# Another order of all steps in a fused linear-attention and gated-MLP kernel, with additions and products exchanged between VectorE and GpSimd

## The chip, the cores and the metric

The kernel runs on one core of a Trainium2 chip. A core has five engines with queues of their own: TensorE (PE in the profile, its weight loads PEld), VectorE (DVE), ScalarE (ACT), GpSimd (POOL) and SyncE (SP), which here issues all DMAs. Each engine works through its own instructions in the order in which they were written, and waits on semaphores for the others. The metric is the time of one launch on the device in microseconds; what is compared is the median of several runs.

## The reference

Eight batches, eight heads, a sequence of 576, heads of 64, a model width of 512 and an MLP of 1024 hidden columns. First a linear attention, with a softmax of q along a head's channels and one of k along the sequence:

```python
q_s = np.exp(q - np.max(q, axis=-1, keepdims=True))
q_s = q_s / (np.sum(q_s, axis=-1, keepdims=True) + 1e-09)
k_s = np.exp(k - np.max(k, axis=2, keepdims=True))
k_s = k_s / (np.sum(k_s, axis=2, keepdims=True) + 1e-09)
kv = np.einsum('bhsd,bhse->bhde', k_s, v)
x = np.einsum('bhsd,bhde->bhse', q_s, kv)      # then heads side by side: 576 x 512
```

Then an MLP with a spatial gate, in float32:

```python
h = x @ w_in
h = 0.5 * h * (1.0 + np.tanh(c * (h + 0.044715 * h ** 3)))
u, v = h[..., :512], h[..., 512:]
v_n = (v - mu) / np.sqrt(var + 1e-06) * g_ln    # mu, var: mean and variance of v's row
v_s = np.einsum('ts,bsd->btd', w_sg, v_n) + b_sg[None, :, None]
out = x + (u * v_s) @ w_out
```

## The kernel before, in words

**Steps and plan.** The kernel is a set of small functions, called steps, and one long text, PLAN, which names all 1254 calls of them in the order in which they are issued. A step's numbers say which piece it works on, most often the batch and then a half, a column block or a row block. A letter at the end chooses the engine where there is a choice: V for VectorE, A for ScalarE, G for GpSimd; without a letter the step's default holds. `InOrder` (line 139) wraps SyncE, VectorE, ScalarE and GpSimd so that each keeps the order of the plan, and `mm` (line 234) does the same for TensorE. So the plan sets the order on every engine, and there is no other scheduler. All instructions of the four wrapped engines carry line 149 in the profile, and all matmuls line 235: groups are told apart by the names of their tiles.

**Precision.** A product in full precision is made of three in a faster format: every operand is split into a high part (suffix _h or _high) and the rest (_l or _low), and high x high, high x low and low x high are summed in PSUM. So each intermediate has a step for its high part (a copy on ScalarE) and one for its low part (a subtraction).

**The stages.** For a batch b:
- k: `load_k`, the maximum over the sequence (`k_ma`, `k_mb`, `k_mc`, then a transpose on TensorE `kt_mm`, `k_top`, and a transpose back `kb_mm`), `k_sub`, `k_exp`; then `kv_mm` with v, `kv_inv` and `kv_scale`. Halves of four heads each.
- q: `load_q`, `q_max`, `q_swapm`, `q_top`, `q_sub`, `q_exp`, `q_sum`, `q_swapd`, `q_inv`, `q_mul`, `q_turn`. A head's 64 channels lie on two groups of 32 partitions; the swaps are four small copies that exchange the maxima (`q_swapm`) or the sums (`q_swapd`) between neighbouring groups. `q_sub` subtracts the maximum, `q_mul` multiplies by the inverse sum, `q_turn` transposes blocks on VectorE.
- x: `x_mm` from kv and q, `x_high` (ScalarE), `x_low` (VectorE).
- The MLP: `hv_mm` (5 row blocks; the tails of two batches share one) with `hv_gelu`, `hv_stat`, `hv_pow`, `hv_norm`, `hv_high`, `hv_low`; `hu_mm` with `hu_gelu`; `sg_mm` over the sequence, `gate`, `gate_high`, `gate_low`; `out_mm`, `out_add`, `out_rest`, `out_store`.

Batch 0 has steps of its own (`k0_...`, `q0_...`, `x0_...`, `hu0_mm`), which work on smaller pieces so as to begin early. Before its MLP the weights must be converted from 64-bit words to the two parts: `wi_a` (ScalarE), `wi_b`, `wi_c`, `wi_d` (VectorE), `wi_h` (ScalarE) and `wi_l`, for eight column blocks of w_in; the same with `wo_` for four blocks of w_out; `ws_h` and `ws_l` for five blocks of w_sg. `wi_x` and `ws_x` let TensorE make the low part where ScalarE then copies it out. The last column block of batch 7 is done in two halves by `last_mm`, `last_add`, `last_rest`, `last_store`.

**Buffers.** PSUM holds three double banks, used in turn (`bank`, line 222) by the x, hu, sg and out products, and two single ones for hv, kv, kt and kb. A step that writes a bank waits until the one three (or two) before it has been read out. q, k and v have two buffers each (one for each half of the heads), so a load waits for the batch before: `load_k` and `load_v` for its `kv_mm`, `load_q` for its `q_turn`. SyncE issues all loads and stores in one queue, and those behind a waiting one wait too.

**Activation tables.** ScalarE's exp steps and gelu steps need different tables; where one kind follows the other in ScalarE's order, a table load stands between them (ACT_TABLE_LOAD in the profile).

## Time and profile before

| | before |
|---|---|
| median of 3 runs | 523.53 us (522.45 to 524.46) |
| the profiled execution | 523.98 us, span of its instructions 522.2 us |
| TensorE busy | 491.4 us (94%), 3862 matmuls |
| VectorE busy | 355.9 us (68%) |
| ScalarE busy | 245.0 us (47%) |
| GpSimd busy | 166.7 us (32%) |
| DMA | 48.74 MB, mean 93 GB/s |

The profile is one execution, with every instruction's start, duration, and, where an engine sat idle before it, what ended the wait. A row of a timeline reads: start, duration, engine, line, operation, tile written <- tiles read, shapes, count, and in brackets the idle time before it with its releaser. A row of a group reads: line, engine, operation, tiles, shapes, count | busy us, mean ns of one | idle time before, and who ended most of it.

### The profile page before, as it was taken

Reading aid. Unit: us, or ns where it says so; the run is one execution under the profiler, and the core shown is the slowest. Engines: PE = TensorE matmul, PEld = TensorE weight load, DVE = VectorE, ACT = ScalarE, POOL = GpSimd, SP = SyncE. Lnnn points to the kernel's source line nnn. Section 1 sums busy time; section 2 is a strip of 40 time slices with the busy share of each in tenths; the row PEclk is TensorE's granted clock in tenths of the full one; section 3 lists DMA queues with packets and bytes.
Section 4 is the critical chain, followed back from the end, with each engine's and each line's share of the span. In section 5 each row is a group of like instructions: output and inputs, shape, how many; then the busy total and the mean of one; then the engine's idle time right before and its main releaser. Section 6 shows DMA issues by size and latency. Waiting matters only on the chain.

```text
span 522.2 us, 9404 instructions
## 1 busy us (share of the span) xinstructions
PE 491.4 (94%) x3862; PEld 447.4 (86%) x3862; DVE 355.9 (68%) x596; ACT 245.0 (47%) x445; POOL 166.7 (32%) x199
## 2 busy tenths in 40 slices
...
GB/s 284 379 279 268 146 150 1 2 187 87 68 130 121 46 137 0 2 102 120 143 1 109 226 75 0 1 1 112 178 97 23 3 68 1 1 0 46 1 17 119
DMA packets 19630, 48.74 MB, mean 93 GB/s; under 512 B 1666, under 2 KB 8196, under 8 KB 19588
## 3 DMA queue, kind: packets, MB, share of 16 engines
...
## 4 chain that ended last, share of the span: by engine, by line
PE 71%; DVE 16%; ACT 5%; DMA 4%; issue 1%; POOL 1%; SPq 1%; ACTq 0%; DVEq 0%; POOLq 0%
PE ps L235 71%; DVE qd L149 3%; DVE ot_i L149 2%; DMA raw_x_l<-w_out 2%; DVE km L149 1%; DVE v L149 1%; DVE qt L149 1%; DMA kk<-k 1%; DVE o L149 1%; DVE ot_o L149 1%; DVE vnl L149 1%; DMA ukt<-k 1%; DVE kk L149 1%; DVE qm L149 1%; ACT v L149 1%
## 5 line engine op out<-in xcount | busy, mean ns | idle before, releaser
L149 POOL TENSOR_TENSOR rs<-ve,half 128x1 f32<-128x1 f32 x36 | 28.9, 810 | 97.0 <-DVE ve L149 94.9
L235 PE MATMUL ps<-ulow,wo_h 128*128 128x288 f32 x256 | 55.7, 296 | 1.1 <-DVE ulow L149 1.1
L235 PE MATMUL ps<-ws_h,vnh 128*128 128x288 f32 x256 | 56.0, 300 | 0.0
L235 PE MATMUL ps<-gh,wo_h 128*128 128x288 f32 x256 | 56.0, 298 | 0.0
L235 PE MATMUL ps<-ws_h,vnl 128*128 128x288 f32 x256 | 55.0, 296 | 0.7 <-DVE vnl L149 0.7
L235 PE MATMUL ps<-gh,wo_l 128*128 128x288 f32 x256 | 55.4, 295 | 0.0
L235 PE MATMUL ps<-ws_l,vnh 128*128 128x288 f32 x256 | 54.8, 295 | 0.0
L149 DVE TENSOR_TENSOR u<-ps,u 128x576 f32<-128x576 f32 x32 | 24.1, 754 | 42.5 <-PE ps L235 34.0
L149 ACT ACT_TABLE_LOAD x28 | 35.9, 1283 | 32.2 <-PE ps L235 21.1
L149 POOL TENSOR_TENSOR ulow<-u,gh 128x576 fp32r<-128x576 f32 x15 | 21.9, 1459 | 91.2 <-DVE ulow L149 46.1
L149 ACT ACTIVATE u<-ps 128x576 f32<-128x576 f32 (+1 forms) x36 | 21.2, 599 | 62.3 <-PE ps L235 62.0
L235 PEld LDWEIGHTS ps<-ws_h,vnh 128*128 128x128 f32 x256 | 41.2, 188 | 2.2 <-DVE u L149 1.8
L235 PEld LDWEIGHTS ps<-ulow,wo_h 128*128 128x128 f32 x256 | 41.2, 188 | 1.6 <-DVE ulow L149 1.3
L235 PE MATMUL ps<-x_h,wi_h 128*128 128x288 f32 x256 | 41.8, 303 | 0.8 <-DVE x_l L149 0.8
L235 PEld LDWEIGHTS ps<-ws_h,vnl 128*128 128x128 f32 x256 | 41.2, 188 | 1.1 <-DVE vnl L149 1.1
L235 PE MATMUL ps<-wi_h,x_h 128*128 128x512 f32 x144 | 40.2, 400 | 1.9 <-DVE kk L149 1.5
L235 PEld LDWEIGHTS ps<-gh,wo_h 128*128 128x128 f32 x256 | 41.3, 188 | 0.6
L235 PEld LDWEIGHTS ps<-ws_l,vnh 128*128 128x128 f32 x256 | 41.3, 188 | 0.0
L235 PEld LDWEIGHTS ps<-gh,wo_l 128*128 128x128 f32 x256 | 41.3, 188 | 0.0
L149 DVE TENSOR_TENSOR o<-ps,x_h 128x576 f32<-128x576 f32 (+1 forms) x33 | 23.7, 730 | 25.4 <-PE ps L235 21.7
L149 ACT ACTIVATE v<-ps 128x512 f32<-128x512 f32 x36 | 21.5, 597 | 40.3 <-PE ps L235 36.8
L235 PEld LDWEIGHTS ps<-x_h,wi_h 128*128 128x128 f32 x256 | 36.0, 190 | 5.0 <-DVE x_l L149 1.7
...
## 6 DMA issues: line engine op xcount, KB each, us to landing
...
```

Of the source, the lines that this page charges most:

```text
L149: ins = op(*args, **kw)
L235: tc.keep_in_program_order(nc.tensor.matmul(*args, **kw))
```

## The change

The plan is replaced by another order of the same 1254 steps; no step is added or left out, and no function changes. 65 of the steps also change their engine:

| steps | from | to | count |
|---|---|---|---|
| `wi_l` 3, 4, 6; `wo_l` 2; `ws_l` 1, 2, 4 | GpSimd | VectorE | 7 |
| `out_rest` | GpSimd | VectorE | 7 |
| `out_rest` | VectorE | GpSimd | 5 |
| `gate_low` | GpSimd | VectorE | 5 |
| `gate_low` | VectorE | GpSimd | 10 |
| `q_mul`, `q0_mul` | GpSimd | VectorE | 6 |
| `q_mul` | VectorE | GpSimd | 5 |
| `q_sub`, `q0_sub` | GpSimd | VectorE | 3 |
| `q_sub` | VectorE | GpSimd | 2 |
| `q_swapm`, `q_swapd`, and q0's (six of these in batch 0) | GpSimd | ScalarE | 12 |
| `q_swapm` 2 0 and 3 1, `q_swapd` 3 1 | ScalarE | GpSimd | 3 |

The diff, cut to the head (up to the first `hu_mm`), one stretch of the middle and the tail:

```diff
...
-load_q0 1 0, q0_max 1 0, load_q0 0 0, q0_max 0 0, load_k0 3, q0_swapm 1 0 G, q0_top 1 0, q0_sub 1 0, load_k0 0, k0_max 3, k0_exp 3, q0_exp 1 0
-k0_max 0, load_q0 1 1, q0_max 1 1, q0_swapm 0 0 G, q0_top 0 0, q0_sub 0 0, q0_sum 1 0, load_q0 0 1, q0_max 0 1, load_k0 2, k0_max 2, load_b, b_h
-q0_swapd 1 0 G, q0_inv 1 0, q0_exp 0 0, q0_sum 0 0, load_eye, q0_swapm 0 1 G, q0_top 0 1, load_w_in 3, wi_a 3, wi_b 3, k0_exp 2, q0_mul 1 0, load_k0 1
-k0_exp 0, k0_max 1, k0_mm 0, q0_swapm 1 1 G, q0_turn 2 0, wi_c 3, k0_exp 1, q0_top 1 1, q0_turn 3 0, load_w_in 1, wi_a 1, wi_b 1, load_w_in 0
-k0_copy 0, wi_a 0, q0_swapd 0 0 G, q0_inv 0 0, k0_mm 1, q0_sub 1 1, wi_d 3, k0_mm 2, load_v 0 1, wi_b 0, k0_copy 2, load_v 0 0, wi_c 1, wi_c 0
-q0_sub 0 1, k0_mm 3, k0_copy 3, q0_exp 0 1, load_w_in 2, q0_sum 0 1, k0_copy 1, load_w_in 5, wi_d 1, load_w_in 7, q0_exp 1 1, kv_mm 0 1, kv_mm 0 0
-kv_inv 0 1, q0_mul 0 0, wi_h 1, wi_d 0, kv_scale 0 1, load_w_in 4, x0_mm 1 0, neg, kv_inv 0 0, wi_a 2, q0_sum 1 1, q0_swapd 0 1 G, wi_b 2, wi_h 0
-wi_x 0, wi_h 3, q0_inv 0 1, x0_high 1 0, x0_neg 1 0, wi_l 1, load_w_sg 3, load_k 1 0, wi_c 2, wi_l 3, wi_a 7, wi_a 5, kv_scale 0 0, q0_mul 0 1
-q0_turn 0 0, q0_turn 1 0, wi_d 2, x0_mm 0 0, wi_h 2, q0_turn 1 1, wi_x 2, x0_high 0 0, x0_neg 0 0, wi_b 5, q0_swapd 1 1 G, x0_low 1 0 A, load_k 1 1
-q0_inv 1 1, q0_mul 1 1, wi_b 7, load_w_in 6, x0_low 0 0 A, q0_turn 0 1, wi_l 0 A, load_w_sg 0, hu0_mm 1 0, load_q 1 0, hu0_gelu 1 0, hu0_mm 3 0
-wi_c 5, wi_a 6, q0_turn 3 1, q0_turn 2 1, load_q 1 1, k_ma 1 0, load_w_out 1, load_v 1 0, hu0_gelu 3 0, x0_mm 1 1, wi_c 7, load_g, wi_a 4
-load_w_out 0, wi_d 5, x0_mm 0 1, x0_high 0 1, hu0_mm 0 0, x0_high 1 1, x0_neg 1 1, load_w_out 2, x0_neg 0 1, wi_h 5, load_w_out 3, wi_x 5
-x0_low 1 1 A, wi_l 2 A, ws_h 0, load_w_sg 1, wi_l 5 A, b_l, k_mb 1 0, x0_low 0 1 A, k_mc 1 0, kt_mm 1 0, hu0_mm 2 0, q_max 1 0, wi_d 7, wi_h 7, wi_x 7
-k_ma 1 1, wo_a 1, k_top 1 0, kb_mm 1 0, hu0_gelu 0 0, k_mb 1 1, wi_b 4, k_mc 1 1, wi_c 4, hu0_gelu 2 0, q_max 1 1, ws_x 0, load_w_sg 4, q_swapm 1 0 G
-load_w_sg 2, wi_l 7 A, q_top 1 0, wi_b 6, k_sub 1 0, kt_mm 1 1, k_top 1 1, wi_d 4, q_swapm 1 1 G, wo_b 1, q_top 1 1, k_exp 1 0, wi_c 6, wi_d 6
-q_sub 1 0, q_exp 1 0, ws_l 0 A, hu0_mm 2 1, wi_h 6, kb_mm 1 1, k_sub 1 1, wi_h 4, q_sub 1 1, hu0_mm 0 1, q_exp 1 1, q_sum 1 0, q_swapd 1 0, q_sum 1 1
-kv_mm 1 0, wi_l 6, wi_l 4, wo_a 3, kv_inv 1 0, wo_a 0, hu0_mm 1 1, hv_mm 0 1, q_inv 1 0, kv_scale 1 0, wo_b 3, wo_c 3, q_swapd 1 1 G, q_inv 1 1
-wo_b 0, k_exp 1 1, hv_gelu 0 1, wo_c 1, hv_mm 0 3, hv_gelu 0 3, wo_a 2, load_v 2 0, load_v 1 1, kv_mm 1 1, load_k 2 1, q_mul 1 0 1, q_turn 1 1, wo_d 1
-q_mul 1 0 0, wo_c 0, ws_h 3, wo_d 0, hu0_gelu 2 1, kv_inv 1 1, hu0_gelu 0 1, load_k 2 0, q_mul 1 1 0, hv_mm 0 0, hv_gelu 0 0 A, q_turn 1 0, x_mm 1 0
-x_high 1 0, q_mul 1 1 1, x_high 1 1, kv_scale 1 1, wo_b 2, ws_h 2, hu0_gelu 1 1, load_q 2 0, q_turn 1 2, q_turn 1 3, wo_d 3, load_q 2 1, hv_mm 0 2
-wo_c 2, wo_d 2, x_low 1 0, hv_gelu 0 2 A, x_mm 1 1, x_high 1 3, x_high 1 2, x_low 1 1, hv_stat 0 1, hv_norm 0 1, x_low 1 3, wo_h 0, hu0_mm 3 1
-x_low 1 2, hv_pow 0 1, ws_h 4, hv_stat 0 3, hv_mm 0 4, hv_high 0 1, hv_low 0 1, hv_pow 0 3, hv_sq 0 0, hv_mm 1 1, hv_gelu 0 4 A, hv_norm 0 0
-hv_sq 0 2, ws_h 1, hv_stat 0 0 A, hv_mm 1 3, hv_norm 0 3, hv_high 0 3, hv_pow 0 0, ws_l 3 V, hv_low 0 3, hv_sq 0 4, hv_norm 0 4, hv_stat 0 2 A
-hv_gelu 1 1 A, hv_stat 0 4 A, hv_high 0 0, hv_sq 1 1, hv_low 0 0, ws_l 4, hv_pow 0 2, hv_pow 0 4, hv_gelu 1 3, q_max 2 1, k_ma 2 1, hv_norm 0 2
-ws_l 2, hv_mm 1 2, q_max 2 0, ws_l 1, wo_h 1, hv_high 0 2, tail_high 1, hv_low 0 2, tail_high 0, tail_again 0, hu0_gelu 3 1, k_ma 2 0, k_mb 2 0
-hv_gelu 1 2 A, k_mb 2 1, k_mc 2 1, tail_low 0, q_swapm 2 1, hv_stat 1 1 A, wo_h 3, hv_stat 1 3, q_swapm 2 0, q_top 2 0, q_sub 2 0 V, hv_mm 1 0
-tail_low 1, q_top 2 1, hv_gelu 1 0 A, load_v 2 1, k_mc 2 0, q_sub 2 1, q_exp 2 1, sg_mm 0 0, gate 0 0, hv_sq 1 2, kt_mm 2 1, sg_mm 0 2, kt_mm 2 0
-k_top 2 1, kb_mm 2 1, k_top 2 0, wo_l 1, gate 0 2, sg_mm 0 3, hv_norm 1 1, kb_mm 2 0, gate_high 0 0, k_sub 2 1, k_exp 2 1, k_sub 2 0, sg_mm 0 1
-gate 0 1, hu_mm 1 0, hv_norm 1 3, hv_sq 1 0, gate_high 0 2, gate 0 3, gate_high 0 1, wo_h 2, wo_l 0 V, hv_stat 1 0 A, kv_mm 2 1, load_k 3 1, k_exp 2 0
...
-gate 7 0, hu_gelu 7 3, sg_mm 7 1, gate_high 7 0, gate_low 7 0 G, hu_mm 7 1, hu_gelu 7 1, gate 7 1, gate_high 7 1, gate_low 7 1, sg_mm 7 2, sg_mm 7 3
-gate 7 2, gate 7 3, gate_high 7 2, out_store 6 0, gate_high 7 3, gate_low 7 2, gate_low 7 3, out_rest 6 2 V, out_store 6 2, out_mm 7 2, out_add 7 2
-last_mm 7 0, out_mm 7 1, out_rest 6 1, out_store 6 1, last_add 7 0, last_rest 7 0, last_store 7 0, out_add 7 1, out_rest 7 2 V, last_mm 7 1
-last_add 7 1, last_rest 7 1, out_mm 7 0, out_rest 7 1 V, out_store 7 1, last_store 7 1, out_add 7 0, out_store 7 2, out_rest 7 0 V, out_store 7 0
+load_k0 0, k0_max 0, load_q0 0 1, q0_max 0 1, k0_exp 0, q0_swapm 0 1, q0_top 0 1, q0_sub 0 1, load_eye, q0_exp 0 1, load_q0 1 1, load_q0 0 0
+q0_max 1 1, q0_max 0 0, load_w_in 3, q0_swapm 1 1 G, q0_top 1 1, q0_sum 0 1, q0_sub 1 1, q0_swapm 0 0, load_q0 1 0, k0_mm 0, q0_max 1 0, q0_top 0 0
+q0_sub 0 0 V, q0_swapd 0 1, wi_a 3, wi_b 3, load_k0 1, q0_inv 0 1, q0_mul 0 1, q0_exp 0 0, neg, q0_exp 1 1, q0_sum 0 0, q0_swapd 0 0 G, load_w_in 2
+wi_a 2, load_k0 3, k0_max 1, k0_exp 1, q0_sum 1 1, k0_copy 0, q0_inv 0 0, load_v 0 0, wi_c 3, q0_swapm 1 0, k0_mm 1, load_k0 2, load_w_in 1, k0_max 3
+k0_copy 1, k0_exp 3, q0_turn 1 1, wi_b 2, q0_top 1 0, kv_mm 0 0, k0_mm 3, k0_max 2, q0_turn 0 1, kv_inv 0 0, wi_a 1, load_w_sg 0, q0_swapd 1 1
+k0_exp 2, k0_mm 2, wi_c 2, kv_scale 0 0, k0_copy 3, q0_inv 1 1, load_b, q0_mul 1 1 V, wi_b 1, q0_mul 0 0, q0_sub 1 0, x0_mm 0 1, q0_exp 1 0
+load_v 0 1, wi_d 3, q0_turn 0 0, b_h, q0_turn 2 1, load_w_in 0, wi_a 0, k0_copy 2, x0_high 0 1, wi_h 3, q0_turn 1 0, x0_mm 0 0, x0_neg 0 1, q0_sum 1 0
+q0_swapd 1 0, wi_c 1, wi_b 0, load_w_in 7, wi_d 2, load_k 1 0, wi_l 3 V, wi_a 7, wi_c 0, b_l, wi_d 1, wi_h 1, q0_inv 1 0, q0_mul 1 0, kv_mm 0 1
+wi_d 0, kv_inv 0 1, kv_scale 0 1, wi_l 1, wi_h 2, wi_x 2, ws_h 0, load_q 1 0, q_max 1 0, q_swapm 1 0 G, wi_h 0, x0_high 0 0, wi_x 0, q0_turn 2 0
+x0_low 0 1 A, q0_turn 3 0, q0_turn 3 1, k_ma 1 0, x0_neg 0 0, wi_l 2 A, load_w_in 5, x0_low 0 0 A, x0_mm 1 0, x0_high 1 0, load_w_in 4, wi_a 4, wi_b 7
+wi_c 7, wi_d 7, wi_a 5, wi_b 5, ws_x 0, ws_l 0 A, k_mb 1 0, x0_neg 1 0, x0_low 1 0 A, hu0_mm 3 0, hu0_gelu 3 0, load_k 1 1, k_ma 1 1, wi_c 5, wi_d 5
+x0_mm 1 1, x0_high 1 1, wi_l 0 A, wi_h 5, load_w_in 6, wi_a 6, wi_b 4, hu0_mm 2 0, hu0_gelu 2 0, k_mc 1 0, load_w_out 1, k_mb 1 1, k_mc 1 1, load_g
+wi_c 4, x0_neg 1 1, x0_low 1 1 A, wi_b 6, kt_mm 1 0, k_top 1 0, load_q 1 1, wi_x 5, load_w_out 0, wi_l 5 A, wi_h 7, hu0_mm 0 0, kt_mm 1 1, wi_c 6
+hu0_gelu 0 0, wo_a 1, load_w_sg 4, wi_d 4, q_top 1 0, wi_d 6, wi_x 7, k_top 1 1, kb_mm 1 1, load_w_out 2, wi_h 6, q_max 1 1, wi_h 4, q_sub 1 0
+hu0_mm 0 1, k_sub 1 1, wi_l 7 A, load_v 1 0, wi_l 4 V, wi_l 6 V, q_exp 1 0, q_swapm 1 1 G, q_top 1 1, q_sub 1 1, wo_a 0, kb_mm 1 0, k_sub 1 0
+hu0_mm 2 1, q_sum 1 0, wo_b 1, hu0_mm 1 0, k_exp 1 1, wo_b 0, wo_c 1, wo_c 0, wo_d 1, hv_mm 0 0, load_w_out 3, k_exp 1 0, q_exp 1 1, wo_a 3, wo_d 0
+hv_gelu 0 0 A, wo_b 3, hv_mm 0 1, q_sum 1 1, wo_c 3, q_swapd 1 0, hv_gelu 0 1, hv_mm 0 2, q_inv 1 0, q_mul 1 0 0, q_swapd 1 1, hv_stat 0 1
+hu0_gelu 1 0, load_v 1 1, q_inv 1 1, hu0_gelu 0 1, hu0_gelu 2 1, q_turn 1 0, kv_mm 1 1, hv_gelu 0 2 A, kv_mm 1 0, load_k 2 0, kv_inv 1 1, wo_d 3
+hu0_mm 1 1, hv_sq 0 0, q_mul 1 0 1, q_turn 1 1, load_q 2 0, kv_inv 1 0, hv_sq 0 2, kv_scale 1 1, kv_scale 1 0, hv_pow 0 1, wo_h 0, wo_a 2, q_mul 1 1 0
+x_mm 1 0, q_turn 1 2, q_mul 1 1 1, wo_h 1, wo_b 2, wo_c 2, x_high 1 0, wo_d 2, x_high 1 1, hv_stat 0 2 A, hu0_gelu 1 1, q_turn 1 3, load_w_sg 2
+x_low 1 0, x_low 1 1, hv_mm 0 3, hv_gelu 0 3, hv_stat 0 0 A, x_mm 1 1, load_k 2 1, x_high 1 2, hv_norm 0 2, hv_pow 0 0, x_low 1 2, x_high 1 3
+x_low 1 3, hv_norm 0 0, ws_h 2, hu0_mm 3 1, hv_pow 0 2, ws_l 2 V, hv_high 0 2, hv_high 0 0, hv_low 0 0, hv_mm 0 4, hv_norm 0 1, load_w_sg 1
+hv_high 0 1, hv_stat 0 3, k_ma 2 0, hv_low 0 1, k_ma 2 1, k_mb 2 1, hv_mm 1 2, k_mb 2 0, load_q 2 1, k_mc 2 0, hv_pow 0 3, hv_low 0 2, hv_gelu 0 4 A
+hv_sq 0 4, hv_stat 0 4 A, ws_h 1, load_w_sg 3, hv_gelu 1 2 A, hv_norm 0 4, ws_h 3, k_mc 2 1, ws_h 4, hv_mm 1 1, hv_gelu 1 1 A, hv_norm 0 3, hv_sq 1 1
+ws_l 1 V, hv_stat 1 1 A, hv_sq 1 2, hv_mm 1 0, hv_mm 1 3, wo_l 0 V, hu0_gelu 3 1, hv_pow 0 4, hv_stat 1 2 A, hv_high 0 3, ws_l 3 V, hv_low 0 3
+tail_high 0, ws_l 4 V, tail_again 0, tail_low 0, q_max 2 0, q_swapm 2 0 G, tail_high 1, tail_low 1, q_max 2 1, sg_mm 0 3, q_swapm 2 1, hv_gelu 1 0 A
+hv_gelu 1 3, sg_mm 0 0, q_top 2 1, q_sub 2 1, hv_sq 1 0, hv_stat 1 0 A, kt_mm 2 0, k_top 2 0, gate 0 3, gate 0 0, gate_high 0 0, gate_low 0 0 G
+kt_mm 2 1, sg_mm 0 1, k_top 2 1, kb_mm 2 1, load_v 2 0, load_v 2 1, hv_norm 1 2, kb_mm 2 0, k_sub 2 1, k_exp 2 1, gate 0 1, gate_high 0 1, q_top 2 0
+q_sub 2 0, q_exp 2 1, wo_l 1, k_sub 2 0, hv_pow 1 1, sg_mm 0 2, hu_mm 1 0, hv_stat 1 3, k_exp 2 0, kv_mm 2 0, gate_high 0 3, load_k 3 0, q_exp 2 0
...
+kb_mm 4 1, q_swapm 4 1, q_exp 4 0, tail_low 2, sg_mm 2 1, q_top 4 1, k_sub 4 1, k_exp 4 0, k_exp 4 1, load_v 4 0, sg_mm 2 0, q_sum 4 0, q_swapd 4 0 G
+hv_norm 3 0, hv_pow 3 3, hu_gelu 2 2, q_inv 4 0, out_store 1 3, q_mul 4 0 1, hv_norm 3 3, load_v 4 1, kv_mm 4 1, kv_inv 4 1, gate 2 0, out_store 1 2
+kv_mm 4 0, load_k 5 0, kv_scale 4 1, gate 2 1, sg_mm 2 2, gate_high 2 0, gate_low 2 0, q_sub 4 1 V, kv_inv 4 0, hv_mm 3 2, out_store 1 1, q_exp 4 1
+q_sum 4 1, q_mul 4 0 0, gate 2 2, sg_mm 2 3, kv_scale 4 0, k_ma 5 0, k_mb 5 0, q_turn 4 0, hv_gelu 3 2 A, q_swapd 4 1, q_inv 4 1, gate_high 2 2
...
+hu_mm 7 3, sg_mm 7 2, gate 7 2, sg_mm 7 3, gate_high 7 2, hu_gelu 7 3, gate 7 3, gate_low 7 2, gate_high 7 3, gate_low 7 3, out_store 6 2
+out_store 6 3, out_store 6 1, out_mm 7 2, out_add 7 2, out_rest 7 2, out_mm 7 1, out_add 7 1, out_rest 7 1 V, out_store 7 2, out_mm 7 0, out_add 7 0
+out_rest 7 0, out_store 7 1, last_mm 7 0, last_add 7 0, last_rest 7 0, out_store 7 0, last_store 7 0, last_mm 7 1, last_add 7 1, last_rest 7 1
+last_store 7 1
...
```

137 lines of the change are left out of this document (67 added, 70 removed).

## The prediction, made before the changed kernel was run

> **What bounds the kernel now.** I read the page first, then the busy time by stretches, then TensorE's waits and its timeline, and last the timelines of the engines that end its waits.
>
> ```profile
> PE 491.4 (94%) x3862; PEld 447.4 (86%) x3862; DVE 355.9 (68%) x596; ACT 245.0 (47%) x445; POOL 166.7 (32%) x199
> ...
> L149 ACT ACT_TABLE_LOAD x28 | 35.9, 1283 | 32.2 <-PE ps L235 21.1 <-DMA ukt<-k 6.1 <-DVE kk L149 4.5
> ```
>
> TensorE is the bound, and the change leaves it the same 3862 matmuls. So only its idle time can move. The busy time by stretches shows where that lies (columns: stretch, length, then the busy time of each engine):
>
> ```profile
> 0.00:31.00 31.00, 13.33 (x124) 9.05 (x125) 27.72 (x56) 17.61 (x29) 20.66 (x46) 0.96 0.93 320
> 31.00:104.00 73.00, 68.16 (x478) 56.64 (x477) 66.22 (x105) 53.27 (x108) 36.54 (x36) 0.99 0.40 134
> 104.00:517.50 413.50, 409.90 (x3263) 381.69 (x3261) 260.41 (x435) 174.11 (x308) 109.54 (x118) 1.00 0.20 68
> 517.50:522.20 4.70, 0.00 (x0) 0.00 (x0) 1.51 (x2) 0.00 (x0) 0.00 (x0) 0.76 0.43 162
> ```
>
> TensorE idles 17.7 us in the first 31, 4.8 in the next 73, 3.6 in 413.5, and 4.7 after its last matmul. In the first two stretches VectorE is the engine that is nearly full (27.7 of 31, 66.2 of 73), so the head is paced by VectorE's queue. The matmuls that mark the head:
>
> ```profile
> 33.26 0.69 PE L235 MATMUL ps<-x_h,wi_h 128*128 128x288 f32 x4
> ...
> 34.93 1.20 PE L235 MATMUL ps<-qt,kvt 64*64 64x288 f32 x16
> ...
> 42.56 0.70 PE L235 MATMUL ps<-ghws,eye 128*128 128x320 f32 x2
> ...
> 43.93 0.38 PE L235 MATMUL ps<-eye,km 128*128 128x128 f32 x2
> ...
> 52.38 1.17 PE L235 MATMUL ps<-wi_h,x_h 128*128 128x512 f32 x4 [1.54 <-DVE kk L149]
> ...
> 58.81 1.39 PE L235 MATMUL ps<-vv,kk 128*64 128x65 f32 x40
> ...
> 64.74 1.20 PE L235 MATMUL ps<-qt,kvt 64*64 64x288 f32 x16 [1.54 <-DVE qt L149]
> ...
> 75.05 1.09 PE L235 MATMUL ps<-wi_h,x_h 128*128 128x512 f32 x4
> ...
> 77.84 1.09 PE L235 MATMUL ps<-wi_h,x_h 128*128 128x512 f32 x4
> ...
> 104.15 1.22 PE L235 MATMUL ps<-x_h,wi_h 128*128 128x288 f32 x8
> ```
>
> The first hu0_mm has ended at 33.26, where the second starts; that one lasts 1.67 (to 34.93). An hv_mm lasts 2.79 (75.05 to 77.84), ws_x 1.37, an x0_mm 0.6, a kv_mm 1.39. At 104.15 hu_mm 1 0 starts. In both orders the same 52 steps of TensorE stand ahead of hu_mm 1 0, so its start is the measure of the whole head.
>
> Why VectorE is late, with GpSimd's row behind it:
>
> ```profile
> 3.64 1.45 DVE L149 TENSOR_REDUCE qm<-qq 128x18 f32<-128x576 f32 x2 [0.19 <-DMA qq<-q]
> ...
> 15.31 0.43 DVE L149 TENSOR_SCALAR ot_i<-ot_i 128x512 uint32<-128x512 uint32 x1
> ...
> 27.85 0.70 DVE L149 SCALAR_TENSOR_TENSOR ot_i<-raw_vnl,ot_i 128x512 uint32<-128x512 uint32 x1
> ...
> 31.82 0.82 DVE L149 STREAM_TRANSPOSE qt<-qq 128x288 f32<-128x288 f32 x2
> ...
> 48.33 2.50 DVE L149 SCALAR_TENSOR_TENSOR ot_i<-raw_wo_l,ot_i 128x512 uint32<-128x512 uint32 x1
> 50.76 1.47 DVE L149 TENSOR_TENSOR kk<-kk,ps 128x1280 f32<-128x1280 f32 x1
> 52.16 1.34 DVE L149 TENSOR_REDUCE qd<-qq 128x36 f32<-128x1152 f32 x1
> ...
> 56.68 1.15 DVE L149 SCALAR_TENSOR_TENSOR qd<-qd,qe 128x36 f32<-128x36 f32 x1
> ```
>
> ```profile
> 47.78 2.51 POOL L149 TENSOR_TENSOR qq<-qq,qm 128x1152 f32<-128x1152 f32 x1 [1.07 <-DVE qm L149]
> ...
> 56.19 5.58 POOL L149 TENSOR_TENSOR qq<-qq,qd 128x576 f32<-128x576 f32 x4
> ```
>
> The same conversion takes 0.70 at 27.85 and 2.50 at 48.33, while GpSimd works from 47.78 to 50.29: VectorE gets through 0.55 after GpSimd has ended. That is a hold, and what waits behind it is k_sub 1 1 (50.76) and then TensorE at 52.38, its 1.54. The second 1.54, at 64.74, has q_turn late behind pieces like q_inv (1.15) that sat between GpSimd's four q_mul. I put a hold at 1.8 for a q_sub (2.50 less 0.70) and at 0.9 for a q_mul.
>
> **The head, part by part.** Up to the last transposes that the first hu0_mm needs, VectorE's queue in the old order runs from 3.64 to 32.64 (31.82 and 0.82). The new order puts into that part q0_sub 0 0, q0_mul 1 1, wi_l 3 (all three from GpSimd) and a q_max, and takes out wi_b 5, wi_b 7, wi_c 5 and one transpose.
>
> ```profile
> L149 DVE TENSOR_TENSOR qq<-qq,qd 128x576 f32<-128x576 f32 x9 | 6.7, 747 | 0.1
> ...
> L149 DVE TENSOR_TENSOR ws_l<-ghws,ws_h 128x640 fp32r<-128x640 f32 x1 | 0.8, 815 | 0.0
> ```
>
> That is 0.75 + 0.75 + 0.8 + 1.34 - 2 x 0.43 - 0.70 - 0.41 = +1.7, so 34.3. Six exchanges of q leave GpSimd there, and holds with them; I take 0.8 off (half of one hold by a q_sub; bounds 0 and 2): 33.5. Then x0_mm 1 0 to 34.1, and a row of five evacuations on ScalarE (x0_high, two wi_a, ws_l, x0_low) at about 0.65 each:
>
> ```profile
> 29.64 0.64 ACT L149 CAST x_l<-ps 128x576 fp32r<-128x576 f32 x1
> ...
> 47.81 0.67 ACT L149 CAST ws_l<-ps 128x640 fp32r<-128x640 f32 x1
> ...
> 157.47 1.28 ACT L149 ACT_TABLE_LOAD   x1 [6.76 <-PE ps L235]
> 158.76 0.60 ACT L149 ACTIVATE v<-ps 128x512 f32<-128x512 f32 x1
> ...
> L149 ACT COPY qs<-qm 32x36 f32<-32x36 f32 x32 | 7.0, 219 | 10.7 <-DVE qm L149 10.3
> ```
>
> They end at about 37.1, and the first hu0_mm at 37.3 against 33.3. But TensorE has then done more: one x0_mm, one x0_neg and ws_x 0, 0.6 + 0.3 + 1.37 = 2.2. The true lag is 4.0 - 2.2 = **+1.8**.
>
> From there to hu_mm 1 0 the old order needs 104.15 - 33.26 = 70.9 us for about 64.4 us of matmuls (7 hu0_mm 11.7; 9 hv_mm 25.1; 4 sg_mm of 28 matmuls at the 0.139 of an hu0_mm, 15.6; the small ones together 12 by estimate): it loses 6.5, of which 4.8 is plain idle. Now the two places of the new order where VectorE could hold TensorE. hv_mm 0 0 needs wi_l 6, now VectorE's own. From 33.5 that is 28 instructions: eight like 27.85 (5.6), ten like 15.31 (4.3), two at 0.70 for k_ma, a q_max 1.34, k_sub 1.47, two wi_l 1.6, small ones 0.6, in all 16.3. Neighbours overlap by 0.07 (48.33 and 2.50 make 50.83, the next starts at 50.76), so less 2.0, and one hold, plus 1.8: 49.6. TensorE gets there at 37.3 + 5 x 1.67 + 3.9 (an x0_mm, an x0_neg, two wi_x and four transposes, by estimate) = 49.5. A loss of 0.1, and no slack. x_mm 1 0 needs kv_scale 1 0: 28 more instructions, 14.7 (k_sub 1.47, two q_sum 2.7, nine conversions 5.5, two full transposes 1.6, the rest 3.4 by estimate), less 2.0, plus two holds by q_mul, 1.8: 49.6 + 14.5 = 64.1. TensorE is there at 49.6 + 3 x 2.79 + 2 x 1.39 + 1.67 = 62.4. Loss 1.7; the two together, and 0.2 for the smaller waits after them, make 2.0 in place of 6.5: **-4.5**. The bounds are 0 (all hidden) and 6.5 (nothing gained; VectorE's mean of 66.22/105 = 0.63 per instruction, overlaps and holds in it, gives 4.9).
>
> By the Trainium skill, page "SBUF — State Buffer", section "Who interferes with whom", a VectorE instruction with two inputs in SBUF and a GpSimd one that reads SBUF lock each other out for a whole instruction, and reductions do not. The trace agrees (2.50 beside 2.51). Read strictly, wi_l 4 and wi_l 6 on VectorE can now be held as well; two holds more would make the second term -0.9.
>
> **The middle, 104 to 517.** What TensorE waits for there:
>
> ```profile
> PE ps L235 <- DVE x_l L149: 1.2, 2, 0.8
> PE ps L235 <- DVE ulow L149: 1.1, 1, 1.1
> PE ps L235 <- DVE vnl L149: 0.7, 2, 0.4
> PE ps L235 <- ACT v L149: 0.5, 1, 0.5
> ```
>
> 3.5 in six waits. VectorE has 260 of 413.5 busy and GpSimd 110, so five more gate_low on GpSimd, two fewer out_rest, and the exchanged q_mul and q_sub lie beside matmuls. Counting in both orders the matmul work between a producer and its consumer, I find the same tightness: from the last hv_mm of a pair of batches to the first sg_mm 11.2, 11.8, 5.6, 11.6 us before and 11.2, 9.3, 6.0, 6.0 after; bank reuses with less than 3 us of cover, 15 before and 11 after; loads of q and k with under 5 us to their first reader, 5 before and 3 after. Against it stand table switches: reading the gelu and exp steps of ScalarE in order gives 28 before, as the page has, and 32 after, all four extra ones in the middle. That is 4 x 1.28 = 5.1 us of an engine busy 174 of 413.5, and the switch at 157.47 did stand ahead of the 1.1 wait for ulow. I take **0**, with bounds of -3.5 and +5.1.
>
> The Trainium skill, page "ScalarE: Activation LUTs", section "What ACT_TABLE_LOAD costs", has 2.66 us for a switch, a drain included; by it the four cost 10.6 us. The row after 157.47 starts at 158.76, so here a switch is 1.28.
>
> **The tail.** Before, a full block (out_mm 7 0) ends TensorE's work; now it is the second half of last_mm, so the last addition, its rest and the store are of half the size:
>
> ```profile
> L149 DVE TENSOR_TENSOR o<-ps,x_h x5: 448/758/758, 511.1 to 517.5; 128x576 f32<-128x576 f32 x3, 128x288 f32<-128x288 f32 x2
> L149 DVE TENSOR_TENSOR o<-o,x_l x5: 457/750/759, 512.2 to 518.3; 128x576 f32<-128x576 f32 x3, 128x288 f32<-128x288 f32 x2
> ...
> DMA to landing us min/median/max: 1.7/2.1/2.1
> ```
>
> 0.76 + 0.76 become 0.45 + 0.46, and 2.1 becomes 1.7: **-1.0**. out_rest 7 0 on GpSimd ends before the last half does.
>
> **Sum.** +1.8 - 4.5 + 0 - 1.0 = -3.7. The profiled execution took 523.98 (its span 522.2), which gives 520.3; it stands 0.45 above the median of the three runs, 523.53, so the forecast is **519.8**.
>
> **The rivals.**
> 1. VectorE gains nothing: the holds are taken over by the seven conversions now its own, and the 6.5 is lost elsewhere in the head. +1.8 - 1.0 = +0.8: **524.3**. For it: no slack at hv_mm 0 0. Against it: in the new order q_sub 1 0 runs beside a reduction and k_sub, forms of which the timeline has no row drawn out like that of 48.33.
> 2. ScalarE becomes the bound. It gets nine more exchanges (4 x 0.219 = 0.88 each, 7.9) and the four switches (5.1), 13.0 in all; its queue is in order, so a gelu that frees a bank waits behind them. If all of it lay on TensorE's path: 532.8. It decides (slower) from 6.3 on; midway between 6.3 and 13.0 it gives **529.5**. For it: ScalarE's row just ahead of the first hu0_mm, and the waits for ACT v. Against it: 53 of 73 busy in the head.
> 3. More is won: no loss left after the first hu0_mm and no idle in the middle, +1.8 - 6.5 - 3.5 - 1.0 = -9.2: **514.3**.
>
> **Chances.** What this kernel's measurement cannot tell from no change is 0.5%, 520.9 to 526.1. Forecast 0.45 (0.42 of it faster, 0.03 within), first rival 0.22 (within), second 0.18 (slower), third 0.15 (faster). So faster 0.57, within 0.25, slower 0.18. The range reaches 514 to 527.5: below it lies a third of rival 3, above it most of the upper half of rival 2. The forecast's own range is 517 to 523.
>
> **What would show it.** Right: the first hu0_mm ends near 37.3 and hu_mm 1 0 starts near 101.5 (104.15 + 1.8 - 4.5); TensorE's idle time after that is 3 to 4 us; 32 table loads; 3.7 us from the last matmul to the end. The head is wrong if hu_mm 1 0 starts at 104 or later; the middle is wrong if waits for ACT rows exceed 4 us there, or if VectorE shows STT rows above 2 us again in 37 to 64.

## The result, and the profile after

The changed kernel took **510.75 us** (median of 4 runs, 510.08 to 511.26), the kernel before 522.99 beside it (4 runs, 522.29 to 524.46): a ratio of 0.976, interval 0.974 to 0.979. The forecast was 519.8 with a range from 514. The direction was right, but 12.2 us were gained where 3.7 were forecast, and the time lies below the range. The profiled execution took 511.26, its span is 509.5.

The page after, and its busy time by stretches (stretch, length, then the busy time of each engine with its instructions, PEclk, DMA):

```profile
PE 488.1 (96%) x3862; PEld 447.3 (88%) x3862; DVE 342.7 (67%) x602; ACT 258.0 (51%) x485; POOL 144.8 (28%) x157
...
L150 ACT ACT_TABLE_LOAD x32 | 41.1, 1283 | 15.6 <-DVE vn L150 5.3
```

```profile
0.00:31.00 31.00, 14.25 (x130) 9.22 (x132) 25.56 (x59) 23.05 (x54) 12.42 (x23) 1.00 0.90 310
31.00:104.00 73.00, 73.00 (x591) 63.31 (x590) 63.90 (x122) 56.77 (x112) 28.18 (x33) 1.00 0.40 146
104.00:505.00 401.00, 400.23 (x3144) 374.35 (x3143) 252.28 (x420) 178.17 (x320) 104.23 (x103) 1.00 0.20 70
```

TensorE has no idle time at all from 31 to 104 (4.8 before) and 0.8 in 401 (3.6 in 413.5 before). TensorE's timeline at the places that the prediction named:

```profile
28.59 0.49 PE L236 MATMUL ps<-wi_h,minus 128*128 128x512 f32 x1 [1.40 <-ACT wi_h L150]
...
33.33 0.70 PE L236 MATMUL ps<-x_h,wi_h 128*128 128x288 f32 x4
...
35.13 0.71 PE L236 MATMUL ps<-qt,kvt 64*64 64x288 f32 x8
...
47.18 1.11 PE L236 MATMUL ps<-wi_h,x_h 128*128 128x512 f32 x4
...
59.94 1.20 PE L236 MATMUL ps<-qt,kvt 64*64 64x288 f32 x16
...
96.68 1.22 PE L236 MATMUL ps<-x_h,wi_h 128*128 128x288 f32 x8
...
505.36 0.30 PE L236 MATMUL ps<-gh,wo_l 128*128 128x288 f32 x1
```

The first hu0_mm runs from 33.33 to 35.13, hv_mm 0 0 starts at 47.18, x_mm 1 0 at 59.94, hu_mm 1 0 at 96.68. All of it comes without a wait behind 28.59.

To see where the time went, I use one ledger for every kernel below. Each step of TensorE has a length, the median time from its first matmul to the next step's where the next one follows at once. A step's start less the lengths of all steps ahead of it is the time **lost** up to it. (Lengths taken a little differently move the losses in one column by up to 1.8; the differences move by 0.4 at most.)

| lost, us | before | after | difference |
|---|---|---|---|
| at the first hu0_mm | 20.3 | 19.9 | -0.4 |
| from there to hu_mm 1 0 | 7.4 | 0.4 | -7.0 |
| from there to the last matmul | 6.7 | 2.3 | -4.4 |
| last matmul to the end | 4.7 | 3.8 | -0.9 |

Together 12.7, the difference of the spans. The lengths sum to 483.1 in both.

**What changed on VectorE.** In the profile before, rows of VectorE are drawn out beside GpSimd's: the prediction calls this a hold. Four of them, from VectorE's timeline of the kernel before, then GpSimd's rows at the same times:

```profile
11.79 1.11 DVE L149 TENSOR_TENSOR qm<-qm,qs 128x18 f32<-128x18 f32 x1
...
15.65 1.13 DVE L149 SCALAR_TENSOR_TENSOR qd<-qd,qe 128x18 f32<-128x18 f32 x1
...
18.34 1.38 DVE L149 TENSOR_SCALAR ot_i<-ot_i 128x512 uint32<-128x512 uint32 x1
...
24.90 1.25 DVE L149 SCALAR_TENSOR_TENSOR qd<-qd,qe 128x18 f32<-128x18 f32 x1
```

```profile
11.71 1.16 POOL L149 TENSOR_TENSOR qq<-qq,qd 128x576 f32<-128x576 f32 x1
...
15.47 2.39 POOL L149 TENSOR_TENSOR qq<-qq,qm 128x576 f32<-128x576 f32 x2
17.83 1.61 POOL L149 TENSOR_TENSOR qq<-qq,qd 128x576 f32<-128x576 f32 x1
...
23.41 2.70 POOL L149 TENSOR_TENSOR wi_l<-ot_i,wi_h 128x512 fp32r<-128x512 f32 x2
```

The first, second and fourth take 0.17 elsewhere, the third 0.42. I took each VectorE row's length less what its kind takes undisturbed (the lower quartile of its kind in both traces) and summed where that is over 0.15. Ahead of hu_mm 1 0 this is **15.5 us before** (5.7 in seven rows up to 33, 9.8 in ten up to 104) **and 0.6 after** (in two rows, near 55 and 57). Behind hu_mm 1 0 the holds differ little: 14.8 before and 12.1 after. So the new order is free of them in the head alone; behind it TensorE doesn't wait for most of them. VectorE's and GpSimd's timelines after, at the place where wi_l 4 and 6 are made:

```profile
40.48 0.68 DVE L150 SCALAR_TENSOR_TENSOR ot_i<-raw_wo_l,ot_i 128x512 uint32<-128x512 uint32 x1
41.08 0.41 DVE L150 TENSOR_REDUCE kt<-ps 128x2 f32<-128x256 f32 x1
41.42 1.34 DVE L150 TENSOR_REDUCE qm<-qq 128x36 f32<-128x1152 f32 x1
42.67 1.47 DVE L150 TENSOR_TENSOR kk<-kk,ps 128x1280 f32<-128x1280 f32 x1
44.07 1.29 DVE L150 TENSOR_TENSOR wi_l<-ot_i,wi_h 128x512 fp32r<-128x512 f32 x2
```

```profile
40.64 2.51 POOL L150 TENSOR_TENSOR qq<-qq,qm 128x1152 f32<-128x1152 f32 x1 [8.71 <-DVE qm L150]
...
45.54 2.14 POOL L150 TENSOR_TENSOR qq<-qq,qm 128x1152 f32<-128x1152 f32 x1 [1.38 <-DVE qm L150]
```

Beside q_sub 1 0 (40.64) lie two reductions and k_sub, which reads PSUM; the conversions wi_l 4 and 6 (44.07 to 45.36) fit between the two q_sub. Nothing there is drawn out; GpSimd's own row is, from 2.14 to 2.51, behind the conversion that began at 40.48.

### The profile page after: what moved, and what is told of

The parts are those of the page before. It is cut to its first block, busy times and chain, and to the rows that moved or that the text cites. A ratio compares the mean times of both kernels' runs of the same rounds, so it can differ in the third digit from the quotient of the medians.

```text
span 509.5 us, 9412 instructions
## 1 busy us (share of the span) xinstructions
PE 488.1 (96%) x3862; PEld 447.3 (88%) x3862; DVE 342.7 (67%) x602; ACT 258.0 (51%) x485; POOL 144.8 (28%) x157
## 4 chain that ended last, share of the span: by engine, by line
PE 92%; DMA 3%; DVE 3%; SPq 1%; ACT 1%; issue 0%
PE ps L236 92%; DMA qq<-q 1%; DMA kk<-k 1%; SPq L150 1%; DVE ot_i L150 1%; DVE qd L150 0%; DVE qq L150 0%; DVE o L150 0%; DVE qt L150 0%; ACT wi_h L150 0%; ACT ukt L150 0%; DVE x_l L150 0%; DVE km L150 0%; ACT qq L150 0%; DVE k0m L150 0%
## 5 line engine op out<-in xcount | busy, mean ns | idle before, releaser
L150 POOL TENSOR_TENSOR rs<-ve,half 128x1 f32<-128x1 f32 x36 | 26.1, 730 | 121.0 <-DVE ve L150 121.0
L150 DVE TENSOR_TENSOR u<-ps,u 128x576 f32<-128x576 f32 x32 | 23.8, 751 | 52.2 <-PE ps L236 52.2
L150 ACT CAST gh<-u 128x576 fp32r<-128x576 f32 x32 | 21.2, 671 | 46.6 <-DVE u L150 46.5
L150 ACT ACTIVATE vnh<-v,rs 128x512 fp32r<-128x512 f32 x32 | 22.5, 719 | 43.6 <-DVE v L150 36.0
L150 POOL TENSOR_TENSOR ulow<-u,gh 128x576 fp32r<-128x576 f32 x20 | 29.8, 1488 | 44.2 <-ACT gh L150 34.3
L150 POOL TENSOR_TENSOR qq<-qq,qd 128x576 f32<-128x576 f32 x22 | 26.5, 1215 | 53.2 <-DVE qd L150 23.5
```

Source lines behind the costliest of these rows:

```text
L150: ins = op(*args, **kw)
```

## The experiments

Letters in the diffs are engines: V VectorE, A ScalarE, G GpSimd; a step without one has its default. The times of runs made together are compared through the kernel before, run beside them.

**1. Order and engines apart.** One kernel has the new order with the old engine of all 65 steps that changed engine, the other the old order with the new engines.

```
 order:    after's PLAN       engines: before's
-q0_sub 0 0 V, wi_l 3 V, gate_low 4 1 G, q0_swapd 0 1, ...
+q0_sub 0 0, wi_l 3, gate_low 4 1, q0_swapd 0 1 G, ...        (65 steps)
 order:    before's PLAN      engines: after's  (the reverse)
```

> The new order of the steps with the old engine for each of the 65 steps that changed engine. In the traces of before and after, VectorE's rows that are drawn out beside a GpSimd row add up to 15.5 us too much ahead of hu_mm 1 0 before (7 rows up to 33 us, 10 more up to 104) and to 0.7 after. Theory (the order does it: what now lies beside GpSimd's rows are reductions, transposes and reads of PSUM): the sum stays under 4 us, hu_mm 1 0 starts at 96.5 to 98.5, 511 to 514 us. Rival (the engines do it: fewer rows on GpSimd, so fewer holds): with the old engines the holds come back, 8 to 15 us of them, hu_mm 1 0 at 101 or later, 516 to 522 us.

> The old order of the steps with the new engine for each of the 65 steps. Theory (order): holds of 10 us or more stay ahead of hu_mm 1 0, which starts at 102 to 105; 520 to 525 us. Rival (engines): holds of 5 us or less, hu_mm 1 0 at 97 to 100, 514 to 518 us.

Measured: **530.8 us** for the new order alone (ratio 1.015, 1.013 to 1.018) and **539.5 us** for the new engines alone (1.031, 1.029 to 1.034). Both expectations fell, for both theories: the halves alone cost 8 and 17 us, the two together gain 12. The holds came nearer to the theory of order (6.2 us with the new order, between its 4 and the rival's 8; 12.4 with the new engines), but the queues did something else. With the new order and old engines hu_mm 1 0 starts at 105.44. GpSimd has its old exchanges and products again, and q0_sub 1 0 comes at 24.1 instead of 17.8; the 6.2 of holds and a clock at half from 23.8 to 34.0 (last section) lie in the same stretch, and this run doesn't tell the three apart. Far behind, one gate_low shows what a late queue does; TensorE's timeline and busy stretches of that kernel:

```profile
347.78 1.39 PE L258 MATMUL ps<-vv,kk 128*64 128x65 f32 x40
352.48 2.29 PE L258 MATMUL ps<-x_h,wi_h 128*128 128x288 f32 x8 [3.31 <-DVE u L172]
```

```profile
352.50:358.40 5.90, 5.90 (x25) 5.90 (x26) 3.62 (x8) 0.80 (x2) 1.93 (x2) 0.51 0.24 53
358.40:362.00 3.60, 3.60 (x29) 3.60 (x29) 2.29 (x6) 3.47 (x5) 0.67 (x1) 1.00 0.96 362
```

The new order puts gate 4 2, which frees a bank, right behind gate_low 4 1. With gate_low on GpSimd that is harmless; back on VectorE it waits there for its input from ScalarE until 351.00, gate 4 2 stands behind it in the queue until 352.42, and TensorE waits 3.31. Then the matmuls run at a granted clock of 0.51: 2.29 for what takes 1.22 elsewhere. The one wait costs 3.4 + 2.7 = 6.1 in the ledger. With the old order and new engines it is ScalarE's queue; its timeline:

```profile
11.90 0.85 ACT L172 COPY qe<-qd 32x18 f32<-32x18 f32 x4 [0.86 <-DVE qd L172]
12.78 0.68 ACT L172 ACTIVATE qq<-qq 128x576 f32<-128x576 f32 x1
13.49 0.85 ACT L172 COPY qs<-qm 32x18 f32<-32x18 f32 x4
14.36 0.66 ACT L172 ACTIVATE ot_i<-raw_vnl 128x512 f32<-128x512 f32 x1
14.92 2.09 ACT L172 ACTIVATE ukt<-ukt,k0m 128x576 f32<-128x576 f32 x3
```

Two exchanges and a wait for VectorE now stand ahead of k0_exp 2 and k0_exp 0, and the first matmul starts at 16.40 instead of 12.80. That is the head alone: hu_mm 1 0 starts at 107.63, 3.5 later than before. The other 12 are lost behind it in a dozen places, where TensorE's waits name gate_low's tile most often (4.8 us, on VectorE and GpSimd) and then x_low's (2.3); they were not taken apart.

**2. Head and rest apart.** Up to hu_mm 1 0 the one plan, then what is left in the order of the other, each with its own engines.

```
 after's steps up to hu_mm 1 0, then before's remaining steps
 before's steps up to hu_mm 1 0, then after's remaining steps
```

> The new order and engines up to hu_mm 1 0, then the steps that are left in the old order with the old engines. Theory (the three gains lie apart and add: head -7.5, middle -4.4, tail -0.9): hu_mm 1 0 starts at 96.7, the middle loses its 6.7 us again and the end its 4.7, so 516 us (515 to 517.5). Rival (the middle's loss was left over from the late head): 511.5 to 513 us.

> The old order and engines up to hu_mm 1 0, then the steps that are left in the new order with the new engines. Theory (the gains add): hu_mm 1 0 starts at 104.1, after it 2.3 us are lost instead of 6.7, the end is 0.9 shorter: 517.7 us (516.5 to 519). Rival (the new rest is only smooth behind the new head): 520 to 524 us.

Measured: 517.42 (ratio 0.989, 0.987 to 0.991) and 518.19 (0.991, 0.988 to 0.994), that is -5.2 and -4.5 against 522.66 beside them. The new head starts hu_mm 1 0 at 96.45 as expected, the old rest then loses 7.8; behind the old head the new rest loses 2.7. In both, out_mm 0 0 just behind the seam loses 2.2 and 0.9, where it loses under 0.5 in the kernels whose parts belong together; 5.2 + 4.5 + 2.2 + 0.9 is 12.8, about the whole. Both times lie where adding gains put them (515 to 517.5, and 516.5 to 519). So the gains lie apart and add, and the middle was not a consequence of the late head. The end is 3.8 in each kernel with the new order there, whatever its engines (4.7 to 5.3 with the old): that part is the order of the last steps alone.

**3. A hold put in by moving two rows.** wi_l 4 and wi_l 6 move two places in VectorE's queue, so that they lie beside q_sub 1 1.

```
-wi_l 4 V, wi_l 6 V, q_exp 1 0, q_swapm 1 1 G, q_top 1 1, q_sub 1 1
+q_exp 1 0, q_swapm 1 1 G, q_top 1 1, q_sub 1 1, wi_l 4 V, wi_l 6 V
```

> The changed kernel with two rows of VectorE moved by two places: wi_l 4 and wi_l 6 now stand behind q_top 1 1 and so beside GpSimd's q_sub 1 1, instead of just ahead of it; same work, same engines. Theory (a hold is a matter of what lies beside what): one of the two is drawn out from 0.69 to 2 us or more, k_sub 1 0 (45.4) comes 1.5 to 2 later, x_mm 1 0 has 0.1 us to spare and starts 1.2 to 1.7 late, and the total is 511.7 to 512.5 us. Rival (holds cost TensorE nothing, the slack takes them): within 0.4 us of the changed kernel.

VectorE's, GpSimd's and TensorE's timelines of this kernel:

```profile
44.30 3.23 DVE L172 TENSOR_TENSOR wi_l<-ot_i,wi_h 128x512 fp32r<-128x512 f32 x2
47.46 1.48 DVE L172 TENSOR_TENSOR kk<-kk,ps 128x1280 f32<-128x1280 f32 x1
```

```profile
44.47 2.51 POOL L172 TENSOR_TENSOR qq<-qq,qm 128x1152 f32<-128x1152 f32 x1 [0.31 <-DVE qm L172]
```

```profile
53.91 1.20 PE L258 MATMUL ps<-wi_h,x_h 128*128 128x512 f32 x4 [0.96 <-ACT v L172]
...
61.25 0.96 PE L258 MATMUL ps<-qt,kvt 64*64 64x288 f32 x12
```

The pair takes 3.23 instead of 1.29 (the second alone 2.63), k_sub 1 0 starts 2.1 later and x_mm 1 0 1.31 later; hu_mm 1 0 starts at 97.99 instead of 96.68, and the span is 1.2 longer. The delay reaches TensorE earlier than I expected, and through ScalarE: behind the late k_sub 1 0 come k_exp 1 0, a table load and the gelu of hv_mm 0 0 (53.17 instead of 51.64), and hv_mm 0 2 at 53.91 waits for the bank that this gelu reads. The median is 512.18, 1.4 above the changed kernel's; against the kernel before, which read 1.1 higher in this group, the ratio is 0.977 and can't tell. The trace can: the same work in the same engines, the clock at full in both heads, and a hold of 1.9 costs TensorE 1.3, as the theory had it (1.2 to 1.7).

**4. Two kinds of steps back on GpSimd.** The seven conversions, and the six exchanges of batch 0.

```
-wi_l 3 V, wi_l 4 V, wi_l 6 V, wo_l 2 V, ws_l 1 V, ws_l 2 V, ws_l 4 V
+wi_l 3, wi_l 4, wi_l 6, wo_l 2, ws_l 1, ws_l 2, ws_l 4
-q0_swapm 0 1, q0_swapm 0 0, q0_swapm 1 0, q0_swapd 0 1, q0_swapd 1 1, q0_swapd 1 0
+the same six, each with G
```

> The changed kernel with its seven conversions (wi_l 3, 4, 6, wo_l 2, ws_l 1, 2, 4) back on GpSimd; nothing else. Theory (order and engines fit each other as a whole; what counts is that neither VectorE's nor GpSimd's queue is late and that GpSimd's rows lie beside rows they don't hold): wi_l 4 and wi_l 6, 1.28 each on GpSimd, push q_sub 1 1 from 45.5 to about 46.8 and with it kv and q of batch 1, so x_mm 1 0, which has 0.1 us to spare, starts 0.5 to 1.5 late; holds ahead of hu_mm 1 0 rise from 0.7 to 2 to 4 us; 511.5 to 514 us. Rival (VectorE's load is all that matters, it is 4.8 us shorter now): 510 us or less.

> The changed kernel with the six exchanges of batch 0 that it has on ScalarE back on GpSimd (0.8 us each); nothing else. With all 65 old engines the new order had lost 4.5 us more by its first hu0_mm, where GpSimd's q0_sub 1 0 came at 24.1 instead of 17.8. Theory (GpSimd's queue is what was late there): about half of it comes back, the first hu0_mm starts at 34.5 to 36.5 instead of 33.3, 512 to 515 us. Rival (the subtractions, products and conversions made it late, not the exchanges): hu0_mm within 0.5 of 33.3, 510 to 511.5 us.

Measured: 515.33 with the conversions (ratio 0.983, 0.981 to 0.986), hu_mm 1 0 at 101.99; 513.02 with the exchanges (0.979, 0.976 to 0.981), the first hu0_mm at 35.41 and hu_mm 1 0 at 98.78. The exchanges cost what the theory said. The conversions cost more than I expected, and mostly not where I did: x_mm 1 0 comes another 0.7 late, inside my 0.5 to 1.5, but 3.3 are lost by the first hu0_mm already, where wi_l 3 is the only one of the seven. GpSimd's and VectorE's timelines of that kernel:

```profile
25.32 1.28 POOL L172 TENSOR_TENSOR wi_l<-ot_i,wi_h 128x512 fp32r<-128x512 f32 x1 [5.87 <-ACT wi_h L172]
26.68 2.45 POOL L172 TENSOR_TENSOR ws<-vb,ws 1x320 fp32r<-1x320 f32 x2
```

```profile
25.36 1.78 DVE L172 SCALAR_TENSOR_TENSOR ot_i<-raw_vnl,ot_i 128x512 uint32<-128x512 uint32 x1
27.07 2.60 DVE L172 SCALAR_TENSOR_TENSOR ot_i<-raw_vnh,ot_i 128x512 uint32<-128x512 uint32 x2
```

wi_l 3 holds the first of these (0.68 undisturbed), pushes b_l (the two rows on one partition) past it, and b_l holds the next two (1.28 undisturbed): 2.4 us on VectorE from one row moved to GpSimd. In the kernel with the exchanges, holds (2.2 us up to 33) and a later GpSimd stand ahead of the 2.1 lost; this run doesn't tell them apart. In both, the clock falls to half for 3.4 us ahead of the first hu0_mm (last section), which may be a part of the loss.

**5. Rows added on GpSimd.** Seven rows on a spare tile where GpSimd stands idle; the three kernels differ in what such a row does. Nothing reads the tile.

```
+fill(n): G.tensor_tensor(out=t, in0=t, in1=t, op=add)     128x512
      or  G.tensor_copy(out=t[:, 0:256], in_=t[:, 256:512])
      or  G.memset(t, 0.0)
 q0_sub 1 0, +fill, +fill, ... b_l, +fill, +fill, ... q_swapm 1 0 G, +fill, +fill, +fill
```

> The changed kernel with seven rows more on GpSimd where it stands idle in the head (two behind q0_sub 1 0, two behind b_l, three behind q_swapm 1 0): each adds a spare 128x512 tile to itself, and nothing reads the sum. In ten traces all 122 SCALAR_TENSOR_TENSOR rows of VectorE that begin inside a GpSimd row with two inputs are drawn out, by 0.92 us on average; no reduction, transpose, reciprocal or read of PSUM is. Theory (it is the reading of two inputs on both engines): seven holds of 0.5 to 0.95 on VectorE, 4 to 6.5 us of them ahead of hu_mm 1 0 where there are 0.7 now; the first hu0_mm 2 to 3 late, hu_mm 1 0 at 99.5 to 102; 513.5 to 516.5 us. Rival (GpSimd's rows don't matter, VectorE's own queue does): within 0.7 us of the changed kernel.

> As with the seven additions, but each of the seven rows copies one half of the spare tile to the other (one input, 128x256). Theory: the traces have only two such rows beside a row of VectorE with two inputs (the exchanges, 32 partitions), both not drawn out; if one input is enough to hold VectorE, holds of 0.3 to 0.9 each as with the additions; if not, no holds, and within 0.7 us of the changed kernel. I take the first as the likelier, 512.5 to 515 us. Rival: 510.3 to 511.5 us.

> As with the seven additions, but each of the seven rows only writes zeros to the spare tile (no input). Theory (reading holds, not writing, nor the presence of a row): no row of VectorE drawn out by them, hu_mm 1 0 within 0.4 of 96.7, within 0.7 us of the changed kernel. Rival (any GpSimd row of that length holds VectorE): as with the additions, 513 us or more.

Measured: **515.06** with additions (ratio 0.983, 0.980 to 0.986; hu_mm 1 0 at 100.94, 6.2 us of holds), 511.57 with copies (0.977, 0.973 to 0.980; 96.83), 511.0 with zeros (0.976, 0.972 to 0.979; 97.69). VectorE's rows beside fillers, in the kernel with additions, then with zeros:

```profile
34.54 2.85 DVE L173 SCALAR_TENSOR_TENSOR ot_i<-raw_wo_l,ot_i 128x512 uint32<-128x512 uint32 x2
```

```profile
24.12 0.78 DVE L173 TENSOR_SCALAR ot_i<-ot_i 128x512 uint32<-128x512 uint32 x1
...
32.19 1.42 DVE L173 SCALAR_TENSOR_TENSOR ot_i<-raw_wo_l,ot_i 128x512 uint32<-128x512 uint32 x2
```

GpSimd's rows of the fillers, again with additions, then with zeros:

```profile
34.30 3.99 POOL L173 TENSOR_TENSOR sq<-sq 128x512 f32<-128x512 f32 x3
```

```profile
23.52 1.11 POOL L173 MEMSET sq<- 128x512 f32 x2
...
31.93 1.85 POOL L173 MEMSET sq<- 128x512 f32 x3
```

The same pair takes 2.85 beside additions and 1.42 beside writes. So a busy GpSimd is not enough: rows that read two inputs hold the pair, rows that only write don't. The copies (0.40 each undisturbed) held three of VectorE's rows by about 0.2 each and were themselves drawn out to as much as 0.9, which cost TensorE nothing. The time with copies came out close to the rival's 511.5, not where I took it as likelier; what a longer row with one input would hold is not shown.

The additions did what the theory said, in holds, places and time. One wait of TensorE shows it free of the clock, which fell to half from 23.1 to 30.0 in that kernel and was full behind it:

```profile
41.56 0.44 PE L259 MATMUL ps<-eye,km 128*128 128x128 f32 x2 [1.36 <-DVE km L173]
```

This is kt_mm 1 0, which has no wait in the changed kernel. It comes behind the drawn-out pair and one more held row in VectorE's queue, 2.3 of holds. With zeros the time was as expected, but hu_mm 1 0 came 1.0 later than 96.7 where I allowed 0.4; the last section has the likely reason.

One row with a single input, the TENSOR_SCALAR at 24.12, was drawn out beside writes (0.78 against 0.42), against my expectation that none would be. The Trainium skill, page "SBUF — State Buffer", section "Who interferes with whom", has VectorE and GpSimd share a pair of ports: a second SBUF input takes its read side, and a tensor_scalar in a fast mode can take both. The pair beside additions (2.85), the same pair beside writes (1.42) and this TENSOR_SCALAR (0.78) agree with that.

Over the fourteen traces, counting VectorE's rows that begin inside a two-input GpSimd row at least 0.5 us ahead of its end: 161 of 161 SCALAR_TENSOR_TENSOR, 99 of 99 TENSOR_TENSOR with both inputs in SBUF and 14 of 14 TENSOR_SCALAR on 128x512 are drawn out, by 0.75 to 0.96 on average; of 616 reductions, transposes, reciprocals, batch statistics and TENSOR_TENSOR that read PSUM, none. This leaves out GpSimd's hv_pow, which has two inputs but one element a partition: 26 more rows of the first two kinds lie beside one, and none is drawn out.

**6. Holds taken out of the old order.**

```
-wi_d 6, q_sub 1 0, ... hu0_mm 2 1, wi_h 6, kb_mm 1 1, k_sub 1 1
+q_sub 1 0, ... hu0_mm 2 1, kb_mm 1 1, k_sub 1 1, wi_d 6, wi_h 6
-gate_low 1 3
+gate_low 1 3 G
-k_mb 4 0, k_mb 4 1, k_mc 4 1, out_rest 1 1, out_rest 1 2, x_low 3 0
+x_low 3 0, k_mb 4 0, k_mb 4 1, k_mc 4 1, out_rest 1 1, out_rest 1 2
```

> The kernel before with three places changed at which a row drawn out by GpSimd stands ahead of a wait of TensorE: wi_d 6 (2.50 at 48.3) goes behind k_sub 1 1; gate_low 1 3 (2.67 at 164.0, beside q_sub 3 1) goes to GpSimd; x_low 3 0 goes ahead of the two k_mb of batch 4 (1.20 and 1.38 at 181 to 183). Theory (these holds are the waits): the losses at hv_mm 0 1 (1.8), out_mm 1 0 (1.3) and hu_mm 2 3 (0.9) fall to 0.3 or less each; 519.2 to 520.5 us. Rival (the waits pass to the next step): the losses come back within 20 us of each place, 522 to 523.5 us.

Measured: 521.5 (ratio 0.995, 0.993 to 0.997), 2.6 below the kernel before beside it, and between my two expectations. In the middle the loss at out_mm 1 0 falls from 1.3 to 0.5, that at hu_mm 2 3 (0.9) is gone and x_mm 3 1 loses 0.3 more; from hu_mm 1 0 to the last matmul 1.7 less is lost than before. In the head the loss at hv_mm 0 1 only fell from 1.8 to 1.5: wi_h 6 has moved back with wi_d 6, and TensorE's wait now names it.

```profile
51.86 1.21 PE L258 MATMUL ps<-wi_h,x_h 128*128 128x512 f32 x4 [1.20 <-ACT wi_h L172]
```

At the third place the row that I moved was itself the next one due, and the wait passed on. The first of the middle's waits is a hold in plain sight; VectorE, GpSimd and TensorE in the kernel before:

```profile
163.99 2.67 DVE L149 TENSOR_TENSOR ulow<-u,gh 128x576 fp32r<-128x576 f32 x1 [0.52 <-POOL ulow L149]
```

```profile
163.91 2.13 POOL L149 TENSOR_TENSOR qq<-qq,qm 128x1152 f32<-128x1152 f32 x1
```

```profile
166.72 0.53 PE L235 MATMUL ps<-ulow,wo_h 128*128 128x288 f32 x2 [1.06 <-DVE ulow L149]
```

The edit takes this gate_low off VectorE altogether, and so the hold with it. At hu_mm 2 3 the row that TensorE waits for, x_low 3 0, is not held itself but stands behind 3.0 us of holds in VectorE's queue (178.39 to 183.85); the edit moves it ahead of two of the three.

**7. A try at a faster one.**

```
-wi_a 7, wi_c 0, b_l, wi_d 1, wi_h 1, ... wi_h 2, wi_x 2, ws_h 0, ... wi_h 0, x0_high 0 0
+wi_h 2, wi_a 7, wi_c 0, b_l, wi_d 1, wi_h 1, ... wi_x 2, ... wi_h 0, x0_high 0 0, ws_h 0
 (also q_max 1 0 and its exchange behind q0_turn 3 1; x0_high 1 0 ahead of wi_l 2)
```

> The changed kernel with five rows moved in the head, nothing else: wi_h 2 ahead of wi_a 7, ws_h 0 behind x0_high 0 0 and x0_high 1 0 ahead of wi_l 2 on ScalarE; q_max 1 0 behind q0_turn 3 1 on VectorE (and its exchange on GpSimd behind it). TensorE waits 1.40 us for wi_h at 28.6 in the changed kernel while VectorE's rows for it have long ended. Theory (ScalarE's order is what is late there, and VectorE has 0.8 us to spare at 56.3): the first hu0_mm 0.5 to 1.0 earlier than 33.3, hu_mm 1 0 0.4 to 0.8 earlier than 96.7, 510.0 to 510.4 us. Rival (VectorE paces the head up to x_mm 1 0, so the gain is waited away there): the first hu0_mm earlier, hu_mm 1 0 within 0.2 of 96.7, 510.6 to 511 us.

Measured: 511.21 (ratio 0.976, 0.973 to 0.979), no different from the changed kernel. The first hu0_mm starts at 32.75, 0.6 earlier, but the second half of its last third waits for x0_low 1 0, which still stands late in ScalarE's queue; x0_mm 1 1 loses 1.1 and hu_mm 1 0 starts at 97.03. Neither expectation for hu_mm 1 0 (earlier, or within 0.2 of 96.7) held. No kernel here beats the changed one.

## Why the prediction was wrong in size

- **The start, +1.8: wrong, measured -0.3.** The first hu0_mm ended at 35.13, not 37.3: 1.9 later than before, less the 2.2 of extra work. VectorE's last transposes ended at 31.25, not 33.5. The step that failed is "I take 0.8 off (half of one hold by a q_sub; bounds 0 and 2)": the old queue had 5.7 us of holds in that stretch and the new one none, 4.9 more than I took off. Part of that went into longer waits of VectorE for its first inputs (5.4 idle in the first 31 instead of 3.3, so 2.2 more). 33.5 - 4.9 + 2.2 is 30.8, close to 31.25.
- **To hu_mm 1 0, -4.5: right in kind, measured -7.1** (96.68 - 104.15 = -7.5, of which -0.3 above). wi_l 6 came at 45.36, not 49.6: 2.2 from the start, and 1.8 for a hold by q_sub that I priced in and that did not happen. x_mm 1 0 started at 59.94, not 64.1: the same, and the two holds by q_mul came to 0.6, not 1.8. (VectorE has 25 rows up to wi_l 6, not 28; the terms add up to 16.3 all the same.) The bound of 6.5 was also too tight: the ledger makes the loss 7.4. Of the 64.4 of matmul work behind the bound, the four sg_mm were 0.6 too long (3.74 each by the ledger) and the small steps as much.
- **The middle, 0: wrong, measured -4.4.** This is the largest of the errors, half of what the sum missed. The step that failed is "I find the same tightness": I counted matmul work between producers and consumers, without VectorE's rows and what holds do to them, and took the bound of -3.5 from the idle that the profile shows. The ledger shows more than the idle rows, 6.7 against 3.6. The six places where it jumps by over 0.5 make 4.9 of it. Ahead of three of them (out_mm 1 0, hu_mm 2 3 and x_mm 3 1, 3.0 together) stand held rows of VectorE with no idle time behind them; ahead of the other three (kt_mm 3 1, kv_mm 4 1, sg_mm 4 2) none do. Experiment 6 takes back about 1.7 at the first two. For the rest the runs show that it belongs to the new order together with its engines (experiments 1 and 2), not which rows: that stays open.
- **Table loads: right.** 32, as read from the order, and no wait of TensorE for a ScalarE row behind hu_mm 1 0. TensorE's idle time there is 0.8, not the 3 to 4 that I named as a sign of being right.
- **The end, -1.0: right**, 4.7 to 3.8.
- **The rivals.** The first (holds taken over by the conversions) is a real mechanism: experiment 3 gets it by moving two rows, but the new order has them between GpSimd's rows. The second (ScalarE bound) is seen in the head when the new engines meet the old order; how much of the 17 us there is ScalarE's is not shown. The third (more is won) was the nearest at 514.3, and stopped short because its holds and its bound for the middle were those of the sum.

So for the head the mechanism was named (VectorE's rows drawn out by GpSimd) and its size was missed, although all 15.5 us of holds stood in the profile before: I priced two rows and guessed the rest. For the middle no gain was forecast at all. That holds cost TensorE time is shown for single places: put into the new head by two moved rows (experiment 3) and by added rows (experiment 5), and taken out of the old middle (experiment 6). That all 7.5 us of the head come from them is argued from the sums, since no kernel has the old order without its holds. The new head with 0.6, 2.2 and 6.2 us of holds starts hu_mm 1 0 at 96.68, 97.99 and 100.94, and the last of these has the clock in it too.
